# Windowed attention ahead of two expert stages: another order of the blocks in the attention loop

## The chip, the cores and the metric

The kernel runs on one core of a Trainium2 chip. The metric is device time in microseconds (us). Times of the unprofiled runs are given as a median; a profiled execution gives the rows by stretch, engine and instruction.

## The reference

Three stages follow each other. The attention has 4 batches, 8 heads, 576 positions and 64 values a head, with a window of 64 positions behind each one:

```python
scores = scale * np.matmul(q, k.transpose(0, 1, 3, 2))
mask = (rel >= 0) & (rel < 64)             # rel: row less column
scores = np.where(mask, scores, -1e9)
scores = scores - np.max(scores, axis=-1, keepdims=True)
attn = np.exp(scores)
attn = attn / (np.sum(attn, axis=-1, keepdims=True) + 1e-09)
x = np.matmul(attn, v)                     # then rearranged to 2304 tokens x 512
```

Then each token with `x @ w_skip > 0` goes to one of 8 experts, `argmax(x @ w_gate)`, which adds `gate * (relu(x @ w1[e]) @ w2[e])` to it, with `gate` the softmax value of its expert. Last, `h = x @ w_in`, `g = h` where h >= 1, 0 where h <= -1 and `(h + 1)**2 / 4` between, and the output is `g @ w_out`.

## The kernel before, in words

The attention works on 18 tiles of 128 tokens (`NT`); tile t holds one block of 64 positions of two batches. A loop over t = 0 to 16 issues one step for each t, with stages of different tiles in it, so that each engine has work of several tiles. Step 17 is written out behind the loop. The schedule is by hand: each engine takes its instructions in the order of the program, and so do the DMA queues of SyncE (SP), ScalarE (ACT) and GpSimd (POOL).

The blocks of TensorE in a step have these names in what follows, after the helper that issues them, with the shape in which they use the array (rows*columns, as in the profile's rows):

- s (`stage_s`, L343 and L353): four products of a mask and 32 of q and k into two PSUM banks, 64*64. There are three banks, `s0` to `s2`, and tile t takes the banks 2t and 2t + 1, counted modulo 3. Then VectorE reduces each bank to a negated maximum (`nb`, L360), and ScalarE makes eight exponentials of them (`pr`, L364).
- t (`stage_t`, L378): eight transposes of `pr`, 128*128, into the banks `pt0` and `pt1`. They are copied to `pts`, the first by ScalarE (L382) and the second by VectorE (L384); for tiles 15 and 17 ScalarE copies both.
- v (`stage_v`, L406): 32 products of `pts` and v, 128*64, into the bank `o`. VectorE then makes `den`, `rec` and the tile `x` of the attention's output (L412 to L414). At its end `load_v` issues the next values of v on SP's queue.
- x (`stage_x`, L429): four transposes of `x`, 128*128, into the bank that s of that step doesn't take; VectorE copies them to `xT` (L437).
- l (`stage_l`, L450): eight products with `w_gate` and `w_skip`, 128*32, and VectorE's copy `ls` (L458).
- l2 (`stage_l2`, L464): two products that bring the logits into rows, 128*128.

Tokens are given to experts in groups of two to four tiles (`ROUTES`). `route_a` picks the expert on VectorE (six instructions, the last makes `oh`, L485). One step later `route_b` ranks the tokens with products (L500 to L503) and four instructions on VectorE (from `r`, L527), `route_h` makes lists on GpSimd and `route_g` the gates; three steps after `route_a`, `route_c` adds the lists up (products L604). In the loop `route_a` comes in the steps 7, 10 and 13, `route_b` in 8, 11 and 14, `route_c` in 10, 13 and 16. `due` holds the functions that a later step calls.

`scale_q` scales the next q on ScalarE in every odd step. `load_raws` loads weights of the experts, 512 KB each, ahead of time on SP's queue, as long as fewer than `most[0]` of them are held: 1 in the first three steps, 2 up to step 14, 3 from step 15. `work` splits one of them into two halves (a copy on ScalarE, L140, and a difference, L141, on GpSimd within the loop and on VectorE later), at the earliest two steps after its load was seen. The first 14 are listed in `splits`; those that the loop leaves are split by the hooks of experts 0 and 1. The experts then run one after the other, with products L813 and L852, and the last stage has the products L977 and L1006.

Before a step's own blocks, a step of the loop calls

```python
            if t >= 3:
                stage_v(t - 3)
            if t >= 2:
                stage_t(t - 2)
            for f in due.pop(t, ()):
                f()
            if t % 2:
                scale_q(t // 2 + 1)
            stage_s(t)
```

and l2 of tile t - 5, l of t - 4 and x of t - 3 follow.

Of the kernel before, what the change touches and what calls it, by code (L numbers as in the profile page):

```python
# [10 lines left out]
F32 = mybir.dt.float32  # L11
# [5 lines left out]
ALU = mybir.AluOpType  # L17
AX = mybir.AxisListType

P = 128  # L20
# [9 lines left out]
NT = N // P  # L30
# [4 lines left out]
KD = DM // P  # L35
# [19 lines left out]

SLOW = (0, 1, 2, 4, 4, 6, 7, 8, 8)
ROUTES = (3, 3, 3, 4, 2, 3)
WARM = 114
WARM_COLUMNS = 48
PUT_OFF = 98  # L60
WGW = 32
# [12 lines left out]
def moe_chain(  # L74
# [10 lines left out]
    nc = tc.nc  # L85
# [193 lines left out]
    with ExitStack() as actx:  # L279
        ldp = actx.enter_context(tc.tile_pool(name="ld", bufs=2))  # L280
        ap2 = actx.enter_context(tc.tile_pool(name="ap2", bufs=2))
        sm = actx.enter_context(tc.tile_pool(name="sm", bufs=3))
# [32 lines left out]
        st = {"n": []}  # L315
# [14 lines left out]
        def stage_s(t):  # L330


            i, b0 = divmod(2 * t, B)
            m = none if i == 0 else odd if i % 2 else even
            e, o = (i, i - 1) if i % 2 == 0 else (i - 1, i)
            e, o = place[e % 4], place[o % 4]
            s = [bank(f"s{(2 * t + k) % 3}", f"s{2 * t + k}") for k in range(2)]
            for k in range(2):
                for h in range(2):

                    r = slice(h * BLK, (h + 1) * BLK)
                    half = (h + k) % 2
                    nc.tensor.matmul(  # L343
                        s[k][half * BLK : (half + 1) * BLK], lhsT=ident_b[r, r],
                        rhs=m[r].rearrange("p (o k) -> p o k", o=1).to_broadcast([BLK, 4, P]),
                        start=True, stop=False,
                    )
            for p in range(4):
                for k in range(2):
                    for h in range(2):  # L350
                        r = slice(h * BLK, (h + 1) * BLK)
                        half = (h + k) % 2
                        nc.tensor.matmul(  # L353
                            s[k][half * BLK : (half + 1) * BLK, p, :], lhsT=qt[i][r, b0 + k, p, :],
                            rhs=kt[r, e : o + 1 : o - e, b0 + k, p, :], start=False, stop=(p == 3),
                        )
            nb = []
            for k in range(2):
                nb.append(sm.tile([P, 4], F32, tag="nb", name=f"nb{2 * t + k}"))
                nc.vector.tensor_reduce(nb[k], s[k], axis=AX.X, op=ALU.max, negate=True)  # L360
            for k in range(2):
                pr = ap2.tile([P, 4, P], F32, tag="pr", name=f"pr{2 * t + k}", bufs=4)
                for p in range(4):
                    nc.scalar.activation(  # L364
                        pr[:, p, :], s[k][:, p, :], AF.Exp, bias=nb[k][:, p : p + 1]
                    )
                st["p", 2 * t + k] = pr

        def stage_t(t):
            last = t + 1 == NT  # L370
            if last:
                both = ldp.tile([P, 2, 4, P], F32, tag="q", name="pts_last")
            for k in range(2):
                g = 2 * t + k
                pr = st.pop(("p", g))
                pt = bank(f"s{k}" if last else f"pt{k}", f"pt{g}")
                for p in range(4):
                    nc.tensor.transpose(pt[:, p, :], pr[:, p, :], ident)  # L378
                pts = both[:, k] if last else ap2.tile([P, 4, P], F32, tag="pts", name=f"pts{g}")

                if last or k == 0 or t + 3 == NT:
                    nc.scalar.activation(pts, pt, AF.Copy)  # L382
                else:
                    nc.vector.tensor_copy(pts, pt)  # L384
                st["pt", g] = pts

# [35 lines left out]
        def store_t(t, eng):  # L422
            eng.dma_start(x1[t * P : (t + 1) * P, 0:DM], st["x", t])

        def stage_x(t):
            x = st.pop(("x", t))
            px = bank(PX_END.get(NT - t, f"s{(2 * t + 2) % 3}"), f"px{t}")
            for c in range(KD):
                nc.tensor.transpose(px[:, c, :], x[:, c * P : (c + 1) * P], ident)  # L429
            if t + 3 < NT:  # L430
                xT = ap2.tile([P, KD, P], F32, tag="xT", name=f"xT{t}", bufs=1)
            elif t + 3 == NT:
                xT = ap2.tile([P, KD, P], F32, tag="pr", name=f"xT{t}", bufs=4)
            else:
                xT = ap2.tile([P, KD, P], F32, tag="pts", name=f"xT{t}")
            if t + 3 < NT:
                nc.vector.tensor_copy(xT, px)  # L437
            else:
                nc.scalar.activation(xT, px, AF.Copy)
            st["xT", t] = xT  # L440
# [194 lines left out]
        for j, n in enumerate(ROUTES):  # L635
            f = len(of)
            of.update({f + i: (f, i, n, j % 2) for i in range(n)})
        due, since, gates = {}, {}, {}
        for t in range(NT - 1):
            if t >= 3:  # L640
                stage_v(t - 3)
            if t >= 2:
                stage_t(t - 2)
            for f in due.pop(t, ()):
                f()
            if t % 2:
                scale_q(t // 2 + 1)
            stage_s(t)
            if t == 3:
                misc = psp.tile([P, 512], F32, tag="misc", name="misc")  # L650
            most[0] = 1 if t < 3 else 2 if t + 3 < NT else 3
            (load_q if t % 2 else load_k)(t // 2 + 2)
            if t >= 3:
                store_t(t - 3, nc.scalar)
            if t >= 5:
                stage_l2(t - 5, *of[t - 5][1:])
            if t >= 4:
                stage_l(t - 4)
            if t >= 3:
                stage_x(t - 3)  # L660
            if t >= 5:
                tg, i, n, side = of[t - 5]
                if i == n - 1:
                    route_a(tg, n)
                    for f, l in (
                        (partial(route_b, tg, n, side), 1),
                        (partial(route_h, tg, n), 1),
                        (partial(route_c, tg, n), 3),
                    ):
                        due.setdefault(t + l, []).append(f)  # L670
                    gates[t + 1] = partial(route_g, tg, n)
            if t in gates:
                gates.pop(t)()

            if t:
                load_raws()
            for key in raws:
                since.setdefault(key, t)

            if t + 2 < NT and splits and since.get(splits[0][1:], t) + 2 <= t:  # L680
                work(splits, [pool])

        stage_v(NT - 4)
        stage_t(NT - 3)
        stage_s(NT - 1)
        rows = kept(*ROWS_AT, RW)
        nc.gpsimd.memset(rows, 0.0)
        store_t(NT - 4, nc.sync)
# [255 lines left out]
    with ExitStack() as fctx:  # L944
# [181 lines left out]
        for k in range(len(steps) + LAG):  # L1126
# [9 lines left out]
            if k >= LAG:  # L1136
                v, m = steps[k - LAG]
                nb, m0, m1 = VISITS[v]
# [82 lines left out]
```

## Time and profile before

| | us |
|---|---|
| median of 3 runs | 690.89 (690.56 to 696.16) |
| profiled execution, its own time | 695.69 |
| span of the profiled execution | 693.9 |
| busy in the span: TensorE, VectorE, ScalarE, GpSimd | 665.3, 395.9, 425.8, 93.2 |

The span is the time from the first to the last instruction that the profile holds; the execution's own time has some 1.8 us more. All times in rows are counted from the span's start. The attention loop runs from about 5 to 92 us, what follows of the attention and the routing to 114 us, the experts to about 265 us, and the last stage to the end.

### The profile page before, as it was taken

The page shows a single profiled execution, that of the slowest core. Times are in us where ns is not written, and L with a number is a line of the kernel's source. Part 1 is how long each engine was busy: PE and PEld are TensorE (multiplying, and loading weights), DVE is VectorE, ACT ScalarE, POOL GpSimd, SP SyncE. Part 2 cuts the span into 40 slices and gives each one's busy share as a digit, 9 for nine tenths or more (in the row PEclk, how much of TensorE's full clock was granted, in tenths as well). Part 3 has the DMA queues.
Part 4 walks back from the last instruction along what each step waited for, and adds up shares of the span by engine and source line. Part 5 has one row for each costly group of instructions (what it writes and reads, how often), then busy time and mean ns, then how long its engine had stood idle before and what let it go on. Part 6 is the DMA issues. An engine that isn't in the chain of part 4 may idle for free.

```text
span 693.9 us, 12188 instructions
## 1 busy us (share of the span) xinstructions
PE 665.3 (96%) x4633; PEld 571.7 (82%) x4633; DVE 395.9 (57%) x718; ACT 425.8 (61%) x865; POOL 93.2 (13%) x140
## 2 busy tenths in 40 slices
PE   7999889998999989999999999999999999999996
PEld 6777768776777765989899999999999999999995
DVE  5888765897783899786877743333323222322222
ACT  5877653573752774776877666565555565556553
POOL 3256536331311220000000000000000000000000
PEclk9999999999999999999999999999999999999999
DMA  8999755997890883342434003030300030002001
GB/s 237 300 275 287 204 171 186 325 334 277 266 362 30 267 290 127 126 136 92 137 91 137 1 0 77 16 77 16 92 1 0 1 92 0 1 1 46 0 1 45
DMA packets 34583, 88.93 MB, mean 128 GB/s; under 512 B 7014, under 2 KB 8166, under 8 KB 34500
## 3 DMA queue, kind: packets, MB, share of 16 engines
q1 hardware_dynamic: 26352, 74.34, 35.0%
q10 hardware_dynamic: 5748, 6.83, 3.1%
q0 software_dynamic: 2400, 6.68, 2.8%
q8 instruction: 48, 0.79, 0.5%
q14 instruction: 35, 0.29, 0.1%
HBM read 75.91 MB, written 13.12 MB: 128 GB/s over the span
## 4 chain that ended last, share of the span: by engine, by line
PE 54%; ACT 3%; DVE 3%; issue 0%; DVEq 0%
PE h L977 26%; PE po L1006 26%; PE spare L1094 1%; PE p2x L967 1%; DVE c L999 1%; DVE q L992 1%; ACT q L989 1%; ACT gs L994 1%; ACT q L984 0%; ACT q L988 0%; ACT hs L986 0%; ACT w L140 0%; DVE gs L997 0%; DVE c L996 0%; DVE w L141 0%
## 5 line engine op out<-in xcount | busy, mean ns | idle before, releaser
L977 PE MATMUL h<-x2T,w 128*128 128x384 f32 x1152 | 217.7, 337 | 0.4 <-DVE x2T L136 0.4
L1006 PE MATMUL po<-w,gs 128*128 128x512 f32 x864 | 217.0, 395 | 1.1 <-DVE w L141 0.8
L977 PEld LDWEIGHTS h<-x2T,w 128*128 128x128 f32 x1152 | 204.6, 188 | 8.9 <-DVE x2T L136 0.8
L1006 PEld LDWEIGHTS po<-w,gs 128*128 128x128 f32 x864 | 159.5, 188 | 31.4 <-DVE w L141 1.1
L992 DVE TENSOR_TENSOR q<-hs,q 128x384 f32<-128x384 f32 x96 | 53.6, 559 | 178.4 <-ACT q L989 177.9
L984 ACT ACTIVATE q<-h 128x384 f32<-128x384 f32 x96 | 47.0, 489 | 85.6 <-PE h L977 84.4
L994 ACT ACTIVATE gs<-q 128x384 fp32r<-128x384 f32 x96 | 50.4, 525 | 60.3 <-DVE q L992 60.3
L997 DVE TENSOR_TENSOR gs<-q,gs 128x384 fp32r<-128x384 f32 x96 | 53.7, 559 | 44.4 <-ACT gs L994 44.4
L140 ACT ACTIVATE w<-raw 128x1024 fp32r<-128x1024 f32 x64 | 65.4, 1057 | 16.7 <-PEq L924 4.7
L852 PE MATMUL y<-w,hT 128*128 128x512 f32 x264 | 70.1, 403 | 4.2 <-DVE hT L136 2.9
L141 DVE TENSOR_TENSOR w<-raw,w 128x1024 fp32r<-128x1024 f32 x55 | 64.8, 1218 | 3.8 <-ACT w L140 2.1
L852 PEld LDWEIGHTS y<-w,hT 128*128 128x128 f32 x264 | 47.2, 188 | 17.3 <-DVE hT L136 4.6
L989 ACT ACTIVATE q<-q 128x384 f32<-128x384 f32 x96 | 50.4, 525 | 3.0
L988 ACT ACTIVATE q<-q 128x384 f32<-128x384 f32 x96 | 50.5, 526 | 0.0
L364 ACT ACTIVATE pr<-s,nb 128x128 f32<-128x128 f32 x144 | 39.1, 385 | 14.9 <-DVE nb L360 14.9
L986 ACT ACTIVATE hs<-h 128x384 f32<-128x384 f32 x96 | 46.7, 486 | 0.0
L813 PE MATMUL ha<-w,mxT 128*128 128x512 f32 x132 | 33.4, 399 | 3.5 <-DVE mxT L136 0.8
L813 PE MATMUL hb<-w,mxT 128*128 128x512 f32 x132 | 35.0, 399 | 0.0
L813 PEld LDWEIGHTS ha<-w,mxT 128*128 128x128 f32 x132 | 23.9, 188 | 12.2 <-issue 4.5
L777 POOL DMA_INDIRECT x<-mx,idx x11 | 16.5, 1497 | 103.9 <-POOLq L921 39.5
L360 DVE TENSOR_REDUCE nb<-s 128x4 f32<-128x512 f32 x36 | 23.2, 687 | 12.5 <-PE s L353 12.1
L135 ACT ACTIVATE hT<-hTp 128x512 fp32r<-128x512 f32 x22 | 13.1, 598 | 26.3 <-PE hTp L826 13.9
(182 smaller groups left out, 702.7 us busy)
## 6 DMA issues: line engine op xcount, KB each, us to landing
raw<-in_wu SPq DMA_DIRECT2D x62, 512.0 KB
raw<-in_wd SPq DMA_DIRECT2D x31, 512.0 KB
x<-x SPq DMA_DIRECT2D x21, 256.0 KB
vt<-in_vs SPq DMA_DIRECT2D x36, 130.0 KB
out<-out SPq DMA_DIRECT2D x36, 128.0 KB
q<-in_qs SPq DMA_DIRECT2D x8, 512.0 KB
kt<-in_ks SPq DMA_DIRECT2D x8, 512.0 KB
x<-x ACTq DMA_DIRECT2D x16, 256.0 KB
```

The lines of the kernel that those rows point to most:

```text
L140: nc.scalar.activation(t[:, 0], src, AF.Copy)
L141: eng.tensor_tensor(t[:, 1], src, t[:, 0].bitcast(F32), ALU.subtract)
L813: nc.tensor.matmul(ph, lhsT=xT[:, a, c, :], rhs=halves[4 * e + j, c][:, b, :], start=(n == 0), stop=(n == len(seq) - 1),)
L852: nc.tensor.matmul(py, lhsT=hT[j][:, a, c, :], rhs=halves[4 * e + 2 + j, c][:, b, :], start=(j == 0 and n == 0), stop=(j == 1 and n == len ...
L977: nc.tensor.matmul(ph, lhsT=halves[U_IN + m // 4, c][:, b, (m % 4) * P : (m % 4 + 1) * P], rhs=xT[:, a, c, :], start=(n == 0), stop=(n == ...
L984: nc.scalar.activation(q, ph, AF.Relu, bias=0.5, scale=0.5)
L988: nc.scalar.activation(q, q, AF.Relu, bias=1.0, scale=-1.0)
L989: nc.scalar.activation(q, q, AF.Square, bias=1.0, scale=-1.0)
L992: nc.vector.tensor_tensor(q, h, q, ALU.max)
L994: nc.scalar.activation(gs[:, 0], q, AF.Copy)
L997: dve.tensor_tensor(gs[:, 1], q, gs[:, 0].bitcast(F32), ALU.subtract)
L1006: nc.tensor.matmul(po[i], lhsT=gs[:, a, i * P : (i + 1) * P], rhs=w[:, b, :], start=(m == m0 and (a, b) == PASSES[0]), stop=(m == m1 - 1 a ...
```

## The change

The loop's step is put in another order: s first, then the routing products that are due, t, x, l2, l, and v of tile t - 2 at the end (before: v of tile t - 3 at the start, which is the same place counted around the loop). The reductions and exponentials leave `stage_s` and become `stage_m` and `stage_e`; `stage_m(t, 0)` is called between t's transposes and VectorE's copy of the second bank, `stage_m(t, 1)` after it, and the exponentials after both. `xT` gets a second buffer. `load_raws` is called in odd steps only, and in the steps 15 and 16. The warm-up products ahead of the loop are 108 where there were 114. Behind the loop, s of step 17 with its reductions and exponentials is called ahead of t of tile 15.

```diff
-WARM = 114
+WARM = 108
...
-            nb = []
-            for k in range(2):
-                nb.append(sm.tile([P, 4], F32, tag="nb", name=f"nb{2 * t + k}"))
-                nc.vector.tensor_reduce(nb[k], s[k], axis=AX.X, op=ALU.max, negate=True)
+            st["s", t] = s, []
+
+        def stage_m(t, k):
+            s, nb = st["s", t]
+            nb.append(sm.tile([P, 4], F32, tag="nb", name=f"nb{2 * t + k}"))
+            nc.vector.tensor_reduce(nb[k], s[k], axis=AX.X, op=ALU.max, negate=True)
+
+        def stage_e(t):
+            s, nb = st.pop(("s", t))
             for k in range(2):
                 pr = ap2.tile([P, 4, P], F32, tag="pr", name=f"pr{2 * t + k}", bufs=4)
...
-        def stage_t(t):
+        def stage_t(t, between=None):
...
                 else:
+                    if between:
+                        between()
                     nc.vector.tensor_copy(pts, pt)
...
-                xT = ap2.tile([P, KD, P], F32, tag="xT", name=f"xT{t}", bufs=1)
+                xT = ap2.tile([P, KD, P], F32, tag="xT", name=f"xT{t}", bufs=2)
...
         for t in range(NT - 1):
-            if t >= 3:
-                stage_v(t - 3)
-            if t >= 2:
-                stage_t(t - 2)
-            for f in due.pop(t, ()):
-                f()
             if t % 2:
                 scale_q(t // 2 + 1)
             stage_s(t)
+            for f in due.pop(t, ()):
+                f()
+            if t >= 2:
+                stage_t(t - 2, partial(stage_m, t, 0))
+                stage_m(t, 1)
+            else:
+                stage_m(t, 0)
+                stage_m(t, 1)
+            stage_e(t)
...
             if t >= 3:
                 store_t(t - 3, nc.scalar)
+
+            if t >= 3:
+                stage_x(t - 3)
             if t >= 5:
                 stage_l2(t - 5, *of[t - 5][1:])
             if t >= 4:
                 stage_l(t - 4)
-            if t >= 3:
-                stage_x(t - 3)
...
                 gates.pop(t)()
-
-            if t:
+            if t >= 2:
+                stage_v(t - 2)
+
+
+            if t % 2 or t + 3 >= NT:
                 load_raws()
...
-        stage_v(NT - 4)
+        stage_s(NT - 1)
+        stage_m(NT - 1, 0)
+        stage_m(NT - 1, 1)
+        stage_e(NT - 1)
         stage_t(NT - 3)
-        stage_s(NT - 1)
```

## Rows read from the trace of the kernel before

**Rows 1.** Stretches: length, busy us (x instructions) per engine, granted clock, DMA share, GB/s.

```profile
40.00:60.00 20.00, 18.93 (x367) 15.33 (x365) 18.00 (x56) 14.44 (x42) 11.81 (x17) 1.00 1.00 290
...
140.00:160.00 20.00, 18.84 (x88) 14.43 (x87) 19.47 (x24) 14.10 (x18) 5.63 (x8) 1.00 0.97 339
```

**Rows 2.** Instructions in order of time, TensorE, one step: start, length, count.

```profile
46.38 0.41 PE L343 MATMUL s<-mask_even,ident_b 64*64 64x512 bf16 x4
46.62 1.04 PE L353 MATMUL s<-kt,q 64*64 64x128 f32 x32
47.59 0.39 PE L464 MATMUL misc<-quarters,ls 128*128 128x9 f32 x2
...
48.27 0.66 PE L429 MATMUL px<-ident,x 128*128 128x128 f32 x4
48.86 1.16 PE L406 MATMUL o<-vt,pts 128*64 128x65 f32 x32
49.94 1.09 PE L378 MATMUL pt<-ident,pr 128*128 128x128 f32 x8
50.79 0.54 PE L604 MATMUL misc<-at,to 128*128 128x144 f32 x3
```

**Rows 3.** Single lines, 14.4 to 92 us: duration ns min/median/max, first and last start.

```profile
L353 PE MATMUL s<-kt,q x512: 266/269/418, 14.4 to 90.2; 64*64 64x128 f32 x171
L378 PE MATMUL pt<-ident,pr x120: 272/273/477, 16.6 to 89.0; 128*128 128x128 f32 x120
L406 PE MATMUL o<-vt,pts x490: 218/222/309, 15.5 to 92.0; 128*64 128x65 f32 x164
```

**Rows 4.** Instructions in order of time, VectorE, steps 10 and 11.

```profile
55.70 0.19 DVE L485 TENSOR_TENSOR oh<-desc,pick 128x27 bf16<-128x27 f32 x1
...
56.24 0.69 DVE L414 TENSOR_TENSOR x<-o,rec 128x512 f32<-128x512 f32 x1
...
57.54 0.18 DVE L527 TENSOR_TENSOR r<-misc,oh 128x27 f32<-128x27 f32 x1
...
58.31 1.29 DVE L360 TENSOR_REDUCE nb<-s 128x4 f32<-128x512 f32 x2
```

**Rows 5.** Instructions in order of time, three engines, end of the loop.

```profile
88.17 1.09 PE L378 MATMUL pt<-ident,pr 128*128 128x128 f32 x8
89.20 0.41 PE L343 MATMUL s<-mask_even,ident_b 64*64 64x512 bf16 x4
...
97.25 1.22 PE L406 MATMUL o<-vt,pts 128*64 128x65 f32 x32 [1.18 <-ACT pts L382]
...
91.32 2.17 ACT L364 ACTIVATE pr<-s,nb 128x128 f32<-128x128 f32 x8 [1.31 <-DVE nb L360]
...
94.29 0.69 DVE L414 TENSOR_TENSOR x<-o,rec 128x512 f32<-128x512 f32 x1
...
98.95 0.69 DVE L414 TENSOR_TENSOR x<-o,rec 128x512 f32<-128x512 f32 x1
```

**Rows 6.** TensorE's waits 20 to 92 us (total, times, longest); two stretches; a block.

```profile
PE o L406 <- issue: 2.6, 2, 2.0
...
PE misc L464 <- DVE r L527: 0.3, 1, 0.3
...
68.90:72.30 3.40, 1.41 (x33) 1.10 (x32) 2.21 (x9) 2.35 (x10) 1.19 (x1) 1.00 1.02 291
72.40:75.70 3.30, 3.30 (x38) 2.89 (x37) 2.07 (x7) 0.60 (x1) 0.61 (x3) 0.50 0.92 316
...
72.61 1.97 PE L378 MATMUL pt<-ident,pr 128*128 128x128 f32 x8
```

**Rows 7.** Instructions in order of time, TensorE and ScalarE, first steps.

```profile
12.22 1.97 PE L378 MATMUL pt<-ident,pr 128*128 128x128 f32 x8
...
12.70 2.17 ACT L364 ACTIVATE pr<-s,nb 128x128 f32<-128x128 f32 x8 [0.37 <-DVE nb L360]
```

**Rows 8.** Instructions in order of time, ScalarE, expert 1.

```profile
133.49 1.05 ACT L140 ACTIVATE w<-raw 128x1024 fp32r<-128x1024 f32 x1
```

## The prediction

> **What bounds the kernel now.** I read the busy times by stretch first, to see where each engine is full; then TensorE's instructions in order of time through the attention loop, which is what the change rearranges; then VectorE and ScalarE beside them; last the waits, the granted clock and the stage behind. The reader is to see this. In the attention loop TensorE is busy 18.93 of 20 us, VectorE 18.00 and the DMA engines all the time [rows 1]: three resources lie within a tenth of each other, so time taken from one soon belongs to the next. Further on, with the experts, VectorE is fuller than TensorE (19.47 against 18.84 of 20 us) and DMA is at 0.97 [rows 1].
>
> One step of the loop is six blocks of products. By their starts [rows 2]: s 1.21 us (46.38 to 47.59), l2 and l 0.68 together (0.32 and 0.36), x 0.59, v 1.08, and t 0.85 where a routing product follows in the same shape. Where s follows t instead, t takes 1.03 (88.17 to 89.20 [rows 5]), so a plain step is 4.59 us. What a change of shape costs is read at a block's edge: the start of the next block less the last product's start, which is the block's end less one product's duration [rows 3]. s ends at 47.66; less 0.27, its last product starts at 47.39, and l2 at 47.59: 0.20. The edges x to v (48.93 less 0.27 to 48.86) and t to s come out at 0.20 in the same way, and so do l2 to l and l to x. v to t is 49.80 to 49.94, 0.14 to 0.15. Inside one shape t's products start every 0.117 us (1.09 less 0.27, over 7), x's every 0.13; and t to the routing product is 50.76 to 50.79, 0.03.
>
> **The edges.** Before, a step goes v, t, s, l2, l, x: 0.15 + 0.20 + 0.20 + 0.20 + 0.20 + 0.20 = 1.15. After, it goes s, t, x, l2, l, v: s to t 0.20, t to x and x to l2 inside one shape, l2 to l 0.20, l to v 0.20, v to s 0.15. The two new inner edges I take at the transposes' own pitch, 0.12 and 0.13, since a transposition loads a new operand too. That is 1.00, so **0.15 us a step**, and 1.8 us in the twelve steps from s of step 5 to s of step 17. Bounds: an inner edge of 0.03, as from t to the routing product, would give 0.15 + 0.19 = 0.34 a step (4.1 us in all); equal edges would give nothing.
>
> The Trainium skill (TensorEngine Tiling (Array Packing), Tiling Modes, Key Properties) says that changing the tiling mode, and not merely the tile, drains TensorE. The rows bear that out only in part: v to t changes the shape for 0.15, hardly more than the 0.12 to 0.13 between two transposes. By the rule each change left out gives back its whole edge; that is the second rival below.
>
> **What the order ties together.** t of a step now feeds v of the same step, with only x, l2 and l between (0.52 + 0.32 + 0.36 = 1.2 us), and one reduction is put ahead of t's second copy on VectorE. In a plain step that fits. With the step's s at 0, the reduction of bank 0 runs from 1.39 to 2.08, t's last transpose starts at 2.03, its copy runs from 2.38 to 3.06, and v is due at 3.35. The second reduction and xT then end at 4.26, just ahead of the next s at 4.43, which needs that bank.
>
> It does not fit where the step before chose the experts. There `oh` ends at 55.89, and behind it VectorE has den, rec and x, the four instructions from r, then the reductions [rows 4]. After the change, from the end of `oh` to the release of v: den to x 1.04 (55.89 to 56.93), the four instructions 0.77 (57.54 to 58.31), one reduction 0.65 (half of 1.29), the copy 0.68: 3.1 us. TensorE needs from the end of `oh` to v: routing 0.1, t 0.94, x 0.52, l2 0.32, l 0.36, which is 2.24, and `oh` is there 0.1 before the next s ends. **v waits 0.8 us**, and the next s another 0.1 for xT: 0.9, in steps 8, 11 and 14, 2.7 in all. Before, the same spots had waits of their own, near 0.3 for r [rows 6] and 0.3 for `oh`, together about 0.6. So the loop comes out at -1.8 + 2.7 - 0.6 = **+0.3 us**; between -4.1 (inner edges at 0.03, no new wait) and +2.7 (no edge gained).
>
> **The start.** Before, t of step 0 stands at 12.22 and fills the time in which step 1's exponentials run (from 12.70, eight in 2.17 us) [rows 7]. After, s of step 2 stands there, and it needs a bank that the first four of them free at about 13.9. TensorE pauses some 1.7 us. s of step 2 then starts 0.2 earlier than before (14.12), but v of steps 0 and 1 wait for t's copies, 0.8 and 0.4; against that go three edges and a wait of 0.5 that v of step 2 had. I take **+0.2** at s of step 5; bounds 0 and 1.7.
>
> **The end of the loop.** Now `stage_e(NT - 1)` stands ahead of `stage_t(NT - 3)`, whose copies are both ScalarE's: eight exponentials ahead of two copies, the reverse of what the loop does. Before, s of step 17 starts at 89.20, its exponentials end at 93.49, x of step 15 starts at 94.29 and v of step 16 at 97.25, having waited for copies on ScalarE: 8.05 after s [rows 5]. After, from that s: exponentials to 4.29, two copies to 5.4, v of step 15 at 5.45, its x on VectorE 1.70 later as from 97.25 to 98.95 [rows 5], at 7.15; and 2.96 from there to v of step 16 (94.29 to 97.25): 10.1. **+2.05 us**; below 1.0 it can hardly come, since t's 1.03 is all that moved out of the way ahead of that s (it is already counted by comparing at s), above 3 only with a slow clock.
>
> **The raw weights.** Counting through `load_raws` and `work` with `most` and the wait of two steps: before, twelve are loaded in the loop and nine split on GpSimd; after, ten and seven. Two splits, 1.05 us on ScalarE [rows 8] and 1.22 on VectorE each, move behind the attention. One falls in expert 0's last hook, where ScalarE idles; the other in expert 1, ahead of the copy of `h`, where some 0.6 of it shows, and about 0.2 through VectorE. **+0.8**; bounds 0 and 3.1, the time of two loads of 524 KB at 339 GB/s [rows 1], should the experts run short of weights. Six warm-up products fewer, and xT's second buffer, I cost at nothing: TensorE waits for data right behind the first, and the second only lets x stand ahead of l.
>
> **The sum**: 0.3 + 0.2 + 2.05 + 0.8 = +3.3 us. The profiled execution took 695.69 us (span 693.9 and 1.8 around it); the median is 690.89. In it TensorE paused without any wait that the profile shows, 2.6 us ahead of v alone [rows 6], and from 72.4 on the granted clock was 0.50, the 1.2 GHz level, after TensorE had been busy only 1.41 of 3.40 us [rows 6]. All such pauses and that stretch come to some 5.7 us, about what lies between this execution and the median; they are the execution's and not the order's. So I add 3.3 to the median: **694 us**.
>
> **Rivals.** First, the forecast: the dependencies eat the edges, 691.5 to 697. Chance 0.5.
>
> Second, each change left out gives back its whole edge, 0.17 each instead of 0.075 (-4.1 instead of -1.8), and the waits of the three routing steps are covered (-2.7): 694.2 - 5.0 = 689. For it: the 0.03 edge. Against it: x's transposes need a new operand each. By the skill's rule on draining, too, this is the result. Chance 0.22.
>
> Third, the experts run short of weights: 0.8 becomes 3.1, 696.5. It decides once the two late loads reach ScalarE after their turn in expert 2. For it: DMA at 0.97 and VectorE at 19.47 of 20. Against it: TensorE shows no wait there for a split weight now. Chance 0.13.
>
> Fourth, slower: the new pauses bring the clock down. A pause of 2 us did so at 72.4 [rows 6], and the change makes one of 1.7 at the start and one of 2.05 ahead of v of step 15 in every execution. In that stretch the eight transposes of t took 1.97 us [rows 6] against 1.09 [rows 2]; half of its 3.3 us is the most that it costs, 1.5 by the blocks in it. It decides where the granted clock falls behind both and the products there are not waiting anyway: +3.0, with a part of the third, 698 to 699. Chance 0.15.
>
> **How the numbers follow.** The likeliest is the first: 694. The second and the fourth are taken in nearly whole: 687.5 to 698.5. One per cent, about what a measurement of this kernel can tell from no change, is 6.9 us. Faster by more (under 684) needs the second with every pause gone as well: 0.05. Slower by more (over 697.8) is most of the fourth: 0.13. Within: 0.82.
>
> **What would show it.** In the profile after: plain steps of 4.43 us from s to s, with t to x at 0.12; steps 8, 11 and 14 near 5.4, their v waiting for the copy on VectorE; some 10 us from s to v of step 16 at the end, with v of step 15 waiting for ScalarE; seven splits on GpSimd. Wrong would be plain steps near 4.25, routing steps without a wait, or an end of the loop no longer than now.

## The result, and the profile after

The changed kernel took 699.62 us (median of 4 runs, 697.12 to 700.18), the kernel before 691.46 beside it (4 runs, 690.56 to 696.16). The ratio is **1.0100, 95% interval 1.0068 to 1.0132**: 1.0% slower, +6.9 us on 691 (4.7 to 9.1); the medians alone lie 8.2 apart. The profiled execution took 700.18, span 698.4. The forecast was 694.0 (687.5 to 698.5), that is +3.1 on the 690.89 that it was counted from. On that 690.89 the ratio makes 697.8, near the range's upper end; the median itself lies 1.1 above it. So the direction was right, and the size was twice the forecast; of the cases, the fourth rival (slower, 698 to 699) came nearest.

The first profile of before (span 693.9) is one of its longer executions, so the unchanged kernel was profiled once more: 688.77 us, span 687.0. Experiments and times below are each against runs of before on the same chip. The three profiles, cut at the same blocks of TensorE (starts; "experts" is from the first expert product to the end of the last product):

| us | before, first profile | before, second | after |
|---|---|---|---|
| start: up to s of step 5 | 26.40 | 25.67 | 29.52 |
| loop: s of step 5 to s of step 17 | 62.80 | 58.50 | 61.78 |
| s of step 17 to v of step 16 | 8.05 | 8.04 | 10.55 |
| v of step 16 to the first expert product | 17.22 | 15.53 | 15.52 |
| experts and last stage | 574.54 | 574.36 | 576.14 |
| time at a granted clock of 0.50 up to there | 10.2 | 0.0 | 17.1 |

Against the second profile the change costs 3.85 + 3.28 + 2.51 - 0.01 + 1.78 = 11.4 us, the whole difference of the spans. Against the first it seems to save a microsecond in the loop. Both of these executions have a stretch of 3.4 at half clock in the loop (from 72.4 before [rows 6], from 76.4 after) and pauses without a shown wait, and the second profile of before has no such stretch. The loop's length varies by that much in either order: in the seven profiles with the changed loop and its fewer raws it is 58.6 to 63.9, so the 3.28 cannot be put down to the change. The stages below are read from both.

Two stretches of the changed kernel (answer to [rows 1]): length, busy time of TensorE, its weight loads, VectorE, ScalarE and GpSimd, granted clock, DMA share, GB/s.

```profile
40.00:60.00 20.00, 18.31 (x372) 15.97 (x371) 18.04 (x51) 15.43 (x43) 9.63 (x12) 1.00 0.98 275
140.00:160.00 20.00, 18.84 (x88) 14.02 (x87) 19.44 (x24) 15.87 (x20) 5.64 (x8) 1.00 1.00 356
```

TensorE has lost busy time in the loop (18.31 of 20 us, before 18.93) and issued five products more: there is room, and something else sets the pace (step 8, below, lies in it). In the experts ScalarE is fuller (15.87, before 14.10), and DMA too.

**A plain step** (answers to [rows 2]). TensorE's instructions in order of time, changed kernel, step 9: start, length, count.

```profile
49.26 0.41 PE L343 MATMUL s<-mask_even,ident_b 64*64 64x512 bf16 x4
49.47 1.07 PE L353 MATMUL s<-kt,q 64*64 64x128 f32 x32
50.47 1.09 PE L383 MATMUL pt<-ident,pr 128*128 128x128 f32 x8
51.40 0.60 PE L436 MATMUL px<-ident,x 128*128 128x128 f32 x4
51.84 0.29 PE L471 MATMUL misc<-quarters,ls 128*128 128x9 f32 x2
52.05 0.43 PE L457 MATMUL misc<-xT,wg_sb 128*32 128x128 f32 x8
52.41 1.15 PE L413 MATMUL o<-vt,pts 128*64 128x65 f32 x32
53.54 0.41 PE L343 MATMUL s<-mask_odd,ident_b 64*64 64x512 bf16 x4
```

The step takes 53.54 - 49.26 = 4.28 us, where the forecast said 4.43 and a plain step before took 4.59. By starts, t takes 0.93 (before 1.03 with s behind it), x 0.44 (0.59), l2 0.21 (0.32), l 0.36, v 1.13, s 1.21. So the order saves 0.31 a step, twice the forecast: not only the edges go (0.11 each from t to x and from x to l2, against 0.20 with a change of shape), the blocks behind them get shorter too. The two products of l2 last 0.29 instead of 0.39, the four transposes of x 0.60 instead of 0.66. The edge from v to s is 0.20, where the forecast had 0.15.

**A routing step** (answers to [rows 4]). VectorE, then GpSimd, changed kernel, step 8, in order of time.

```profile
45.27 1.34 DVE L546 SCALAR_TENSOR_TENSOR rc<-ps,far 128x3 f32<-128x3 f32 x1
46.65 0.16 DVE L549 SCALAR_TENSOR_TENSOR rc<-rc,ps 128x3 f32<-128x3 f32 x1
46.73 0.68 DVE L362 TENSOR_REDUCE nb<-s 128x4 f32<-128x512 f32 x1
47.33 0.68 DVE L391 COPY pts<-pt 128x512 f32<-128x512 f32 x1
...
44.24 2.36 POOL L141 TENSOR_TENSOR w<-raw,w 128x1024 fp32r<-128x1024 f32 x1 [6.46 <-ACT w L140]
...
48.06 1.15 PE L413 MATMUL o<-vt,pts 128*64 128x65 f32 x30 [1.24 <-DVE pts L391]
```

The first line is an operation on three numbers a partition, and it takes 1.34 us; the next, of the same size, takes 0.16. It ends at 46.61, and the split of a raw weight on GpSimd ends at 46.60. The copy that v needs stands behind it, and v waits 1.24 (last line, TensorE). Step 8 takes 6.75 us, where step 11, with the same work and no split beside it, takes 5.48 (the forecast: near 5.4). This collision stood in no step of the prediction.

The Trainium skill (SBUF — State Buffer, SBUF: two separate sides) says that VectorE and GpSimd share a pair of ports as an exclusive lock, and that a VectorE operation with two inputs in SBUF is shut out for the whole of a GpSimd operation that reads SBUF and began first. `ps` and `far` are two such inputs, and the trace agrees: 1.34 us instead of 0.16, begun 1.03 behind the split and ended with it.

**The start** (answers to [rows 7]). TensorE, then ScalarE, changed kernel.

```profile
11.12 0.40 PE L343 MATMUL s<-mask_odd,ident_b 64*64 64x512 bf16 x2
13.15 0.64 PE L343 MATMUL s<-mask_odd,ident_b 64*64 64x512 bf16 x2 [1.63 <-ACT pr L369]
13.15 2.33 PE L353 MATMUL s<-kt,q 64*64 64x128 f32 x32
15.42 1.97 PE L383 MATMUL pt<-ident,pr 128*128 128x128 f32 x8
...
20.11 0.64 PE L343 MATMUL s<-mask_odd,ident_b 64*64 64x512 bf16 x4
...
11.95 2.17 ACT L369 ACTIVATE pr<-s,nb 128x128 f32<-128x128 f32 x8
```

And two stretches of it, columns as above.

```profile
11.60:21.90 10.30, 8.33 (x106) 7.33 (x110) 3.96 (x8) 6.24 (x19) 0.00 (x0) 0.50 0.73 227
97.00:100.40 3.40, 3.40 (x41) 3.28 (x37) 1.70 (x8) 0.00 (x0) 0.81 (x4) 0.50 0.52 174
```

s of step 2 stops in its middle for 1.63 us, for the bank that the exponentials free; the forecast was 1.7. Just behind the beginning of that pause the granted clock falls to 0.50, the 1.2 GHz level, and stays there for 10.3 us: s takes 2.33 where it takes 1.27 in the second profile of before, t 1.97 against 1.09. There:

```profile
12.38 0.40 PE L343 MATMUL s<-mask_odd,ident_b 64*64 64x512 bf16 x2
13.22 0.40 PE L343 MATMUL s<-mask_odd,ident_b 64*64 64x512 bf16 x2 [0.43 <-DVE pts L384]
13.23 1.27 PE L353 MATMUL s<-kt,q 64*64 64x128 f32 x32
...
16.99 0.41 PE L343 MATMUL s<-mask_odd,ident_b 64*64 64x512 bf16 x4
```

That is TensorE in the unchanged kernel's second profile: s of step 2 at 12.38, of step 3 at 16.99, against 11.12 and 20.11 above. That the pause brings the clock down is not shown: in three other profiles with the same start it falls at 10.5 to 10.7 us, ahead of the pause (which begins at 12.5 to 12.7) and right behind a wait of 2.3 to 2.5 us in the middle of s of step 1, which the old order has too. The second of the two stretches is the other place that the fourth rival named.

**The end of the loop** (answers to [rows 5]). TensorE, ScalarE and VectorE, changed kernel.

```profile
91.30 0.41 PE L343 MATMUL s<-mask_even,ident_b 64*64 64x512 bf16 x4
...
96.18 0.33 PE L413 MATMUL o<-vt,pts 128*64 128x65 f32 x2 [1.51 <-ACT pts L387]
...
101.85 1.22 PE L413 MATMUL o<-vt,pts 128*64 128x65 f32 x32 [0.49 <-ACT pts L387]
...
93.47 2.17 ACT L369 ACTIVATE pr<-s,nb 128x128 f32<-128x128 f32 x8 [1.59 <-DVE nb L362]
95.48 1.13 ACT L387 ACTIVATE pts<-pt 128x512 f32<-128x512 f32 x2
...
98.90 0.69 DVE L421 TENSOR_TENSOR x<-o,rec 128x512 f32<-128x512 f32 x1
```

From s of step 17 to v of step 16 it is 10.55 us; the forecast was 10.1. v of step 15 waits for the two copies behind the eight exponentials, and starts 4.88 after s, not 5.45; but it and what follows run at the low clock (97.0 to 100.4), so x of step 15 starts later than forecast (7.60 after s, not 7.15).

**TensorE's waits** (answers to [rows 6]), changed kernel, 20 to 92 us: in total, times, longest.

```profile
PE o L413 <- issue: 2.6, 1, 2.6
PE o L413 <- DVE pts L391: 1.7, 2, 1.2
```

The pauses without a shown wait are here as before (2.6 against 2.6). New is the wait of v for VectorE's copy, where the forecast put it. In the experts, ScalarE's halves of the splits behind the attention (answer to [rows 8]; count, then shortest, median and longest in ns):

```profile
L140 ACT ACTIVATE w<-raw x57: 1038/1052/1067, 117.1 to 257.0; 128x1024 fp32r<-128x1024 f32 x57
```

There are two more than before (55), at the same 1.05 us. The first product of the third tile comes 0.7 later, counted from the first tile's, than in the second profile of before, of the fourth 1.5, and the whole is 1.78 longer. That is not this profile's alone: experts and last stage take 576.1 to 577.1 in seven of the eight profiles with fewer raws (the eighth has pauses of its own, below), and 574.4 to 575.2 in the six with all of them.

### The profile page after: what moved, and what is told of

The parts are those of the page before. It is cut to its first block, busy times and chain, and to the rows that moved or that the text cites. A ratio compares the mean times of both kernels' runs of the same rounds, so it can differ in the third digit from the quotient of the medians.

```text
span 698.4 us, 12182 instructions
## 1 busy us (share of the span) xinstructions
PE 665.8 (95%) x4627; PEld 575.0 (82%) x4627; DVE 399.5 (57%) x720; ACT 427.7 (61%) x865; POOL 89.2 (13%) x138
## 4 chain that ended last, share of the span: by engine, by line
PE 53%; DVE 4%; ACT 3%; issue 0%; DMA 0%; DVEq 0%; ACTq 0%
PE po L1022 26%; PE h L993 25%; PE spare L1110 1%; PE p2x L983 1%; DVE c L1015 1%; DVE q L1008 1%; ACT q L1005 1%; ACT gs L1010 1%; DVE w L141 1%; ACT q L1000 0%; DVE c L1012 0%; ACT hs L1002 0%; ACT q L1004 0%; DVE gs L1013 0%; DMA x<-x 0%
## 5 line engine op out<-in xcount | busy, mean ns | idle before, releaser
L141 DVE TENSOR_TENSOR w<-raw,w 128x1024 fp32r<-128x1024 f32 x57 | 67.2, 1217 | 4.4 <-ACT w L140 2.2
L369 ACT ACTIVATE pr<-s,nb 128x128 f32<-128x128 f32 x144 | 40.6, 372 | 7.0 <-DVE nb L362 5.3
L413 PE MATMUL o<-vt,pts 128*64 128x65 f32 x544 | 23.3, 234 | 6.9 <-issue 3.0
```

The lines of the kernel that those rows point to most:

```text
L141: eng.tensor_tensor(t[:, 1], src, t[:, 0].bitcast(F32), ALU.subtract)
```

## The experiments

My theory after the result: the order itself, in the loop, neither gains nor loses, and the 6.9 us are the sum of three things at its rims: the start, the end of the loop, and the raw weights. The rival: the loop's new waits and the clock are what costs. All ratios are to the kernel before, with 95% intervals of about 0.003 (2 us) either way. Where nothing else is said an edit is made to the changed kernel.

**The start alone taken back.** t of tile 0 again ahead of s of step 2:

```diff
+            if t == 2:
+                stage_t(0)
             stage_s(t)
...
-            if t >= 2:
+            if t >= 3:
                 stage_t(t - 2, partial(stage_m, t, 0))
```

> The changed kernel with t of tile 0 back ahead of s of step 2; all else as changed. Theory A (the order at the start costs the time: with s of step 2 there, TensorE pauses, and the granted clock stays at 0.50 from 11.6 to 21.9 us): s of step 5 starts near 26.5 us instead of 29.5, the 0.50 stretch there lasts 3.4 us instead of 10.2, and the time falls by some 3 us, to 696 to 697. Rival B (the long stretch comes of the six warm-up products left out, or of data that land later, and would be there in either order): s of step 5 stays at 29 or later and the time within 1 us of 699.6.

Measured 697.0, ratio 1.0057 (1.0027 to 1.0087): 3.0 us less than the changed kernel's 1.0100. s of step 5 came at 27.21. The stretch at half clock did not shrink to 3.4 as theory A had it; it lasted 6.8 (9.5 to 16.4).

**The end of the loop alone taken back.** `stage_t(NT - 3)` ahead of `stage_e(NT - 1)`; s of step 17 stays ahead of both:

```diff
-        stage_e(NT - 1)
         stage_t(NT - 3)
+        stage_e(NT - 1)
```

> The changed kernel with the exponentials of tile 17 behind t of tile 15 and its two copies on ScalarE. Theory A (eight exponentials ahead of two copies hold v of tile 15 back): from s of step 17 to v of tile 16 it takes near 8.3 us instead of 10.55, and the time falls by 2 us, to 697.5. Rival B (VectorE's chain from the second reduction through the expert choice decides there, whatever ScalarE does): v of tile 15 starts earlier, v of tile 16 doesn't, and the time stays within 0.7 us.

Measured 700.16, ratio 1.0084 (1.0048 to 1.0120): 1.1 less. s of step 17 to v of step 16 fell from 10.55 to 8.68, so 1.9 comes back at that place, and the granted clock did not fall there. Behind it 0.66 is lost in this profile: v of step 16 to the first expert product took 16.18 instead of 15.52. That is not the edit's, since the profiles with the start and the raws taken back, whose end is the changed kernel's, have it too (16.23 and 16.17), and the kernel with all three parts taken back, below, which has this edit, does not (15.53).

**The raw weights alone taken back.**

```diff
-            if t % 2 or t + 3 >= NT:
+            if t:
                 load_raws()
```

> The changed kernel with a raw weight asked for in every step from 1, as before the change. Theory A (two splits fewer cost the experts 1.5 us, and GpSimd's split at 44 us holds VectorE's rc back by 1.2): nine splits on GpSimd, experts 1 and 2 lose nothing against before, and the time falls by 1.5 to 2.7 us, to 697 to 698. Rival B (the loop is short of DMA, so that more raw weights lengthen TensorE's pauses without a shown wait): the pauses in the loop grow by 2 us or more and the time doesn't fall.

Measured 696.5, ratio 1.0058 (1.0034 to 1.0083): 2.9 less. In its profile steps 8, 11 and 14 take 5.56, 5.48 and 5.49; there is no long operation on VectorE. The split that lay beside the ranking of step 8 now runs from 38.61 to 40.99, in step 7, since raws that come in every step are split in other steps. Experts and last stage take 574.79, as before.

**All three taken back**, the three diffs above together. What is left is the new order in the loop, with the 108 warm-up products, `xT`'s second buffer and s of step 17 ahead of t.

> The changed kernel with three undone parts together: t of tile 0 ahead of s of step 2, the exponentials of tile 17 behind the copies of tile 15, a raw weight in every step. Theory A (the three costs are separate: measured alone they gave back 0.4, 0.2 and 0.4 per cent): ratio to before 1.000 (0.996 to 1.004), that is the order of the loop itself gives about what its new waits take. Rival B (they are one cost, the DMA and clock state of the loop, given back by any of them): ratio 1.005, no better than the best alone.

Measured 692.16, **ratio 0.9999 (0.9973 to 1.0025)**. The three single savings add up to 3.0 + 1.1 + 2.9 = 7.0, and together they are 7.0 (1.0100 less 0.9999, on 691). So the order in the loop costs nothing that this interval shows (1.8 us either way), and the 6.9 us are in the three. How they divide is less sure: a difference of two such ratios is uncertain by some 3 us, and 1.1 alone could be nothing. That the sum meets 7.0 to the tenth is chance, since the changed kernel's ratio, with its own interval, stands in all three. The stages of the profiles (2.5 for the end of the loop, 1.8 for the experts) put the costs in the same places. It leaves the question why a step that is 0.31 shorter gives nothing. The stretch from s of step 5 to s of step 17, first the unchanged kernel's second profile, then this kernel:

```profile
25.67:84.17 58.50, 57.07 (x1103) 46.53 (x1103) 50.21 (x136) 45.83 (x127) 33.51 (x35) 1.00 0.99 286
```

```profile
27.54:86.00 58.46, 54.91 (x1103) 47.54 (x1102) 50.51 (x135) 46.23 (x124) 33.57 (x35) 1.00 0.96 275
PE o L413 <- DVE pts L391: 1.4, 3, 0.5
PE o L413 <- issue: 1.3, 1, 1.3
PE o L413 <- ACT pts L387: 0.5, 2, 0.2
```

TensorE is busy 2.16 us less (57.07 to 54.91), and idle 2.12 more (1.43 to 3.55). 1.9 of the idle time is v waiting for copies; the rest is mostly a pause of 1.3 in one step without a shown wait. So the loop's sum came out as forecast (-0.04 against +0.3), out of larger parts; that they cancel so closely is in part luck, in one profile of each.

**Can the waits in the routing steps be had for less?** On the kernel with all three taken back, the routing products behind t instead of ahead of it, so that VectorE copies first:

```diff
-            for f in due.pop(t, ()):
-                f()
...
             else:
                 stage_m(t, 0)
                 stage_m(t, 1)
+            for f in due.pop(t, ()):
+                f()
             stage_e(t)
```

> As the run with the three undone parts, and the routing products that are due come behind t and its copies instead of ahead. Theory A (in steps 8, 11 and 14 v waits because the four instructions of the ranking stand ahead of the reduction and the copy on VectorE): these steps fall from 5.48 us to near 4.7 and the time by 2 us against that run. Rival B (v would wait there for x of the step before, or the next s for xT, just as long): the steps stay above 5.2.

Measured 693.81, ratio 1.0024 (1.0001 to 1.0048). TensorE's waits in its loop:

```profile
PE misc L471 <- DVE r L534: 2.7, 3, 0.9
PE misc L471 <- DVE acc L615: 2.6, 3, 0.9
```

Steps 8, 11 and 14 take 5.53 to 5.54: rival B's times, by a wait that it did not name. The wait moved from v to l2, which writes the PSUM tile `misc` that the ranking still reads: 0.9 in steps 8, 11 and 14, and 0.9 in the steps that place the tokens (10, 13, 16) as well.

And, on the same kernel, the second copy of tiles 6, 9 and 12 on ScalarE:

```diff
+                if between and k and t in (6, 9, 12):
+                    between()
+                    nc.scalar.activation(pts, pt, AF.Copy)
-                if last or k == 0 or t + 3 == NT:
+                elif last or k == 0 or t + 3 == NT:
```

> The kernel with start, tail and raws as before and the new order in the loop, in which the second copy of the turned weights of blocks 6, 9 and 12 is ScalarE's work instead of VectorE's, in the steps 8, 11 and 14 that rank. Theory A (v waits there for VectorE's copy, which stands behind the ranking): steps 8, 11 and 14 fall from 5.5 to between 4.6 and 5.0 us, the time falls by 1.5 to 2.5 us against the kernel without this copy, ratio 0.996 to 0.998 against the kernel before. Theory B (the copy on ScalarE runs before its exponentials, and these then come late for the next t): steps 9, 12 and 15 grow by what 8, 11 and 14 lose, ratio 0.999 to 1.001.

Measured 693.43, ratio 1.0018 (0.9993 to 1.0043; single runs 689.99 to 698.3). TensorE's waits in its loop:

```profile
PE o L416 <- ACT pts L390: 4.1, 3, 2.5
PE o L416 <- DMA vt<-in_vs: 2.0, 2, 1.7
```

Steps 8, 11 and 14 fell to 4.34, 4.89 and 4.89, as theory A said. The time didn't follow: v now waits elsewhere, 1.7 for its own load in step 6, and 0.86, 2.46 and 0.77 for ScalarE's first copy in steps 7, 9 and 15. In step 9 that copy stands behind the split of a raw weight, ahead of which ScalarE stood still for 2.26 (the weight's load was issued at 45.40, the split began at 51.59). Step 9 takes 7.49 and step 15 5.42, where they take 4.62 and 4.60 without the edit; step 12 takes 4.35 (4.47). So two of the three steps that theory B named did grow, but by a wait of v, not of t. This is one profile; whether each run loses it in the same places is open.

**The raw weights alone, in the old order.** The edit is made to the kernel before:

```diff
-            if t:
+            if t % 2 or t + 3 >= NT:
                 load_raws()
```

> The kernel before with raw weights loaded only in the odd steps and in steps 15 and 16, nothing else changed. Theory A (the raws are a cost of their own, a split of pair 13 that falls to ScalarE and VectorE inside expert 1 and later weights): +1 to +2 us, ratio 1.0015 to 1.003, the start and the loop as before. Theory B (the raws cost mainly because the split on GpSimd then falls beside VectorE's ranking, as in steps 8 and 14 of the changed kernel): +2 to +4 us, with an operation of L546's kind of over 1 us in the loop. Theory C (nothing, the experts find their weights in time): within 0.5 us.

Measured 693.19, ratio 1.0017 (0.9998 to 1.0036). Experts and last stage took 576.25, 1.9 more than in the second profile of before; so theory A's cost is there in the profile, and the interval in time allows nothing to 2.5 us. The collision is there too; VectorE and GpSimd, step 8:

```profile
45.17 1.12 DVE L539 SCALAR_TENSOR_TENSOR rc<-ps,far 128x3 f32<-128x3 f32 x1
...
43.91 2.36 POOL L141 TENSOR_TENSOR w<-raw,w 128x1024 fp32r<-128x1024 f32 x1 [9.17 <-ACT w L140]
```

Again it ends with the split (46.29 and 46.27). But in the old order v doesn't stand behind it: step 8 takes 5.19 instead of 4.91, 0.3 more, where in the new order the same collision costs 1.27.

**What the start costs: clock or pause?** First the six warm-up products given back:

```diff
-WARM = 108
+WARM = 114
```

> The changed kernel with 114 warm-up products, as before the change. Theory A (the six products are worth nothing by themselves): the time within 2 us of 699.6, ratio 1.010. Rival B (where the program's instructions lie decides how long TensorE pauses after the branches of the experts, which 40 products more had made several us long): the pauses ahead of the experts' first products change by several us and the time by more than 3 us.

Measured 699.73, ratio 1.0091 (1.0061 to 1.0120): nothing that can be told from the changed kernel. Then TensorE kept at work ahead of s of step 2, with 40 small products:

```diff
+            if t == 2:
+                more = psp.tile([P, H, P], F32, tag="o", name="more")[:, 0, 0:WARM_COLUMNS]
+                for _ in range(40):
+                    nc.tensor.matmul(more, lhsT=ones, rhs=ones[:, 0:WARM_COLUMNS], start=True, stop=True)
             stage_s(t)
```

> The changed kernel with 40 products of the warm-up's kind ahead of s of step 2, so that TensorE isn't idle while the exponentials of tile 1 run; the order stays as changed. Theory A1 (the clock is what the start costs): the granted clock is back at 1.00 by 15 us, s of step 5 starts near 27.3, the time falls by 2 us, to 697.5. Theory A2 (the order itself is what it costs, the clock little): the clock comes back early, but s of step 5 starts at 28.5 or later and the time falls by less than 1 us.

Measured 717.82, ratio 1.0335: far from both. The start is not where it was lost (s of step 5 at 28.14). TensorE's waits in the experts:

```profile
PE ha L833 <- PEq L941: 13.4, 4, 4.7
PE ha L833 <- issue: 4.3, 1, 4.3
```

Ahead of the first products of an expert's tile, behind the jump at L941, TensorE stands still for up to 4.7 us, which it does nowhere in the changed kernel. Two runs with other fills, at the same number of TensorE instructions as the changed kernel, narrow down what does it. Eight products of 512 columns:

```diff
-WARM = 108
+WARM = 100
...
+            if t == 2:
+                more = psp.tile([P, 4, P], F32, tag="o", name="more")
+                for _ in range(8):
+                    nc.tensor.matmul(
+                        more, lhsT=ones, rhs=ones.rearrange("p (o k) -> p o k", o=1).to_broadcast([P, 4, P]),
+                        start=True, stop=True,
+                    )
             stage_s(t)
```

> The changed kernel with 8 products of 512 columns ahead of s of step 2 and 8 warm-up products fewer, so that TensorE has as many instructions as the changed kernel. Theory A1 (the clock is what the start costs): no pause at the experts' branches, the stretch at 0.50 ends by 18 us, s of step 5 starts at 27 to 28 and the time falls by 1 to 2 us. Theory A2 (the order is what it costs): s of step 5 at 28.4 or later, as in the changed kernel, whatever the clock does, and the time stays.

Measured 698.28, ratio 1.0070 (1.0037 to 1.0102). No such pauses. s of step 2 to s of step 3 took 4.19 at full clock, instead of 6.96 from 13.15 to 20.11; but s of step 2 stood at 16.44, and s of step 5 came at 29.20, no earlier. By itself that does not decide, since the second half of s of step 1 was late as well (11.96 against 10.08, behind a wait of 4.07 for ScalarE instead of 2.19). Counted from that half, s of step 5 comes 17.24 later here, 18.05 to 19.44 in the four kernels with this start and no fill, 15.71 to 16.95 in the four with t of tile 0 back, and 15.52 to 16.74 in the three profiles of the old order. So the fill gives back part, and the order at the start keeps the rest. And the 40 small products again, with 40 fewer at the very beginning:

```diff
-WARM = 108
+WARM = 68
```

> The changed kernel with 40 small products ahead of s(2) and 40 fewer at its very beginning, so that TensorE has as many instructions as in the changed kernel. Theory A (the long pauses at the experts' branches with 40 more products came from where TensorE's instructions lie, not from the products): no pause of over 2 us at the experts' jumps, time 698 to 701. Theory B (they come from the products themselves): the pauses stay, 712 to 718.

Measured 697.55, ratio 1.0094 (1.0058 to 1.0131), no pauses at the jumps: theory A. The pauses came with 40 more instructions on TensorE and went when 40 others were taken out, with the same products in the same place. s of step 5 stands at 28.24 there, 17.34 behind the second half of s of step 1. That the place of the code behind the jump sets them is what is left of the causes that I had; no row shows it directly.

**The kernel before once more.**

> The kernel before, unchanged, profiled once more, since its first profiled execution took 5 us more than its median. Theory A (the executions differ by stretches of half clock): fewer or other stretches at 0.50 than the three of the first profile, and a time of 690 to 693 that differs by half the length of the stretches missing. Theory B (they differ in the experts, by weights that come late): the same stretches, and the difference after 114 us.

Measured 688.77, below the 690 to 693 expected. Theory A: no stretch at 0.50 in it at all, and from the first expert product on the two agree within 0.2 us. Of the 6.7 us between them up to there, at most 5.1 are the low clock (half of 10.2), and less where TensorE waits anyway: the stretch of 3.4 at the start makes 0.73. The rest I put down to the first profile's pauses without a shown wait (2.6 ahead of v and 0.8 ahead of t in its loop, against 0.5 ahead of v in the second).

## Where the prediction was right and where it was wrong, by its own steps

**The edges** were mis-sized, to the good side: 0.31 a plain step instead of 0.15. The forecast took an edge as the gap between two blocks; the measured gain has the first products of the next block in it as well (l2 and x above). The second rival's size for them (0.17 an edge, 0.34 a step) was the nearer one, and 4.28 is close to the 4.25 that the prediction itself named as a sign of being wrong. The Trainium skill's rule on draining (TensorEngine Tiling (Array Packing), Tiling Modes, Key Properties) fits this step better than I granted: t to x and x to l2, without a change of mode, follow at 0.11, and the step loses 0.31 for two changes fewer.

**The new waits of v** were right in place and cause, and in what the step takes: step 11 at 5.48 against near 5.4, v waiting for VectorE's copy behind the ranking (the profile shows 0.44 of it as a wait, the forecast had 0.8). The forecast for the loop, +0.3, held in the kernel that has the new order alone (58.46 against 58.50). Its bounds of -4.1 and +2.7 leave out the 0.6 that the middle value takes off; with it they are -4.7 and +2.1. The second rival, which needed these waits covered, fell.

**The start** is the step that failed: "I take +0.2 at s of step 5". The pause itself was right (1.63 against 1.7). But I offset it against the first profile's s of step 2 at 14.12, in an execution whose t just ahead of it had taken 1.97 at half clock [rows 7]; in the second profile, at full clock, it stands at 12.38. And the low clock was put into the fourth rival alone. s of step 5 comes at 28.43, 28.45, 28.45 and 29.52 in the four runs with this start and nothing added to it but a few warm-up products, and at 25.67, 26.40 and 27.06 in the three of the old kernel: +2.05 by the medians, 3.0 in time by the first experiment. In the four kernels with t of tile 0 back it comes at 26.58 to 28.02, so by the medians 1.1 of the 2.05 goes with t's place, and what the rest goes with is open. The low clock there lasts 6.8 to 10.2 us with this start, 0 to 3.4 in the old order, and 3.4 to 6.8 with t of tile 0 back; it falls ahead of the new pause in three profiles of four, so how much of the cost is the clock's stays open too.

**The end of the loop**: mechanism right, 2.5 instead of 2.05, the rest being the low clock from 97.0 to 100.4: the three kernels with the fills, which have the same end and no fall of the clock in it, take 9.94 to 9.95, near the forecast's 10.1. In time, the exponentials put back behind the copies gave 1.1, in an interval that reaches from nothing to the whole.

**The raw weights**: +0.8 was too small twice. In the experts they cost 1.8 (576.14 against 574.36); the two splits were counted, seven being left on GpSimd as forecast, but I let most of their time hide behind ScalarE's idle time. And the splits that stay came to lie beside the ranking, in step 8 of the profile, for 1.27 there, and in step 14 as well in four of the other kernels with this order. I counted how many instructions move, not beside what they come to lie. In the eight kernels with fewer raws there are 13 such long operations, and each ends with a split, within 0.03 us. Taken back, the raws give 2.9.

**The cases.** The fourth rival named both places of the low clock (11.6 to 21.9 and 97.0 to 100.4) and gave 698 to 699; it had a chance of 0.15. Its cause is shown only in part: at the end of the loop the clock fell in four of the seven profiles that have this wait of v, at the start mostly ahead of the pause. With the terms of the start and the end it made 0.2 + 2.05 + 3.0 = 5.2 us of the two, and taking both back gave 3.0 + 1.1 = 4.1; that it met the time is partly luck, since the raws' 2.9 make up the rest. The first, with 0.5, had the loop right and the rims wrong. The third, a shortage of weights in the experts, came true in a small part: TensorE waits there once, 0.4, for a split weight, and before it did not.

Open are the pauses of TensorE without a shown wait, which come in different steps of each execution, and why the kernel with the second copies on ScalarE loses its gain.

## What to carry to other kernels

A new order in a loop is judged where it begins and ends as much as inside: here the loop's own sum was zero within 2 us, and the fill at its start, the drain at its end and the moved weights cost what the change cost. When work is thinned or moved to other steps, look at what the other engines do at the step where it lands; a weight split that came to lie beside VectorE's tiny instruction cost 1.27 in that step, not much less than the 1.8 of the two splits that moved behind the loop. And take a second profile of the kernel before ahead of any subtraction: two executions of the same program differed by 6.7 us in the stage in question.

## What the runs showed of the hardware that I had not expected

- A VectorE operation on 128x3 numbers took 0.74 to 1.43 us instead of 0.16 while GpSimd split a weight, once or twice in the loop of each of the eight kernels with fewer raws, and in none of the six profiles with all of them.
- Forty more small products on TensorE at the start made it pause up to 4.7 us at jumps more than 100 us later (717.82 against 697.55 with as many taken out elsewhere).
- A block that follows without a change of the array's shape is shorter inside as well: l2's two products 0.29 instead of 0.39, x's four transposes 0.60 instead of 0.66.
